# The guard of the softmax sums moved to ScalarE, the gelu of v kept in PSUM for its statistics, the early scaling by ScalarE

## The chip, the cores and the metric

The program runs on one core of a Trainium2 chip. A core has five engines that work through their own instruction queues in order: TensorE (PE; its weight loads are shown as PEld), VectorE (DVE), ScalarE (ACT), GpSimd (POOL) and SyncE (SP), which here only issues transfers. The metric is the device time of one execution in microseconds, as a median over runs.

## What is computed

For 8 batches of 8 heads with 576 positions and a head size of 64, causal attention with a bias that grows with a running sum of relu(s), and behind it a gated feed-forward network (gMLP) on the 512 columns that the 8 heads of a batch make:

```
cum    = cumsum(max(s, 0))
scores = q @ k.T / 8 + min(-(cum_i - cum_j), 0), masked causally
attn   = exp(scores - max);  attn = attn / (sum(attn) + 1e-9)
x      = attn @ v                              # 8 heads side by side: 576 x 512
h      = gelu_tanh(x @ w_in);  u, v = h[:, :512], h[:, 512:]
v_n    = (v - mean(v)) / sqrt(var(v) + 1e-6) * g_ln
out    = x + (u * (w_sg @ v_n + b_sg)) @ w_out
```

All of it is float32. From the ninth head on, float32 products are made of rounded parts (a high and a low part of each operand).

## The kernel before

**Attention, a head at a time.** `scores` makes five row tiles of scores in PSUM (`sc`, lines 295 to 298), VectorE adds the mask, writes the tile to SBUF (`p`) and takes its row minimum (`mn`, line 305), ScalarE takes the exponential in place and sums its rows into a column of `sum` (line 315, an ACTIVATE and an accumulator read). There are two sets of `p` tiles, used by even and odd heads. `norm` then adds 1e-9 to the five columns of sums (line 320, VectorE, 128x5), takes the reciprocal (`rs`, line 321, VectorE) and multiplies the `p` tiles by it in place (line 335). Which engine multiplies is read from a table, `ENG`: all five tiles by GpSimd from head 12 on (`'n': 'ggggg'`); in heads 0 to 11 the fourth entry of `'n0': 'gggvg'` gives the 128x448 tile to VectorE. `transposes` turns `p` on TensorE (`pt`, line 374), ScalarE and VectorE copy the result out of PSUM (`pa`, `pb`, `pd`), and `pv` multiplies it with v (`xx`, line 447) into `xr`.

**Feed-forward, a batch at a time.** `ffn(b)` starts when its eight heads are done and runs beside the next eight. It consists of units, each with a PSUM tile: five `v` units (`vm`, 128 or 64 rows by 512), and eight each of `u` (`um`), `s` (`sm`) and `o` (`om`, 128x288). All of them take their PSUM tile from one pool of three buffers (`ps_m`, tag `m`). A unit's tile is free for another unit when its last reader is through. In a `v` unit, `gelu2` runs Square (ScalarE, line 490), a multiply (VectorE, 491), Tanh (ScalarE, 492) and a last multiply (VectorE, 493), which is the last reader of `vm` and writes to the SBUF tile `vt`. Behind it come the statistics (`BN_STATS` line 535, `BN_AGGR` line 536), five small steps on GpSimd for one over the root (`rt`, lines 538 to 543), and `(vt - mean) * g_ln` on VectorE (line 544, inputs `vt` and `g_b`). From that, `vn` is made as a high part (ScalarE, 552) and a low part (GpSimd, 554 and 555; for the 64-row unit VectorE). The `s` units need `vn` of all five `v` units.

**What sets the order.** `place` gives each step a due time counted in heads, and the steps are run in that order to give the program. Within that, a scheduler that replays the program with its own costs (`schedule_with_timeline_sim=True`) decides in which order each engine's queue gets its instructions. An edit of one instruction can therefore change the order on all engines.

Of the kernel before, what the change touches and what calls it, by code (L numbers as in the profile page):

```python
# [13 lines left out]
AF = mybir.ActivationFunctionType  # L14
ALU = mybir.AluOpType
# [9 lines left out]
CH = S // 2  # L25
# [23 lines left out]
U2 = 7  # L49
ENG = {'k': 'sg', 'vs': 'sg', 'xs': 'gg', 'ln': 'sg', 'gt': 'sg', 'w': 'gg', 'ws': 'sv', 'n': 'ggggg', 'n0': 'gggvg', 'ws1': 'g'}  # L50
MT = 52.0
# [8 lines left out]
def tile_attn_gmlp(  # L60
# [12 lines left out]
    nc = tc.nc  # L73
# [244 lines left out]
    def norm(h, its, rs):  # L318
        c = slice(min(its), max(its) + 1)
        nc.vector.tensor_scalar(out=rs[:, c], in0=sums[h % 2][:, c], scalar1=1e-9, scalar2=None, op0=ALU.add)  # L320
        nc.vector.reciprocal(out=rs[:, c], in_=rs[:, c])  # L321
        for it in its:
# [11 lines left out]
            for po, pi, f in o:  # L334
                e.tensor_scalar(out=po, in0=pi, scalar1=f, scalar2=1.0, op0=ALU.mult, op1=ALU.mult)  # L335

# [144 lines left out]
    def ffn(b):  # L481
# [6 lines left out]

        def gelu2(ps, t, n):
            nc.scalar.activation(out=t, in_=ps, func=AF.Square)  # L490
            nc.vector.scalar_tensor_tensor(out=t, in0=t, scalar=1.0 / GA, in1=ps, op0=ALU.add, op1=ALU.mult)
            nc.scalar.activation(out=t, in_=t, func=AF.Tanh, scale=GC * GA)
            nc.vector.scalar_tensor_tensor(out=t, in0=t, scalar=1.0, in1=ps, op0=ALU.add, op1=ALU.mult)  # L493

        vn = {}

        def v_unit(tt, _):
# [30 lines left out]
            if tt == NT:  # L528
                nc.scalar.copy(out=t, in_=ps[r:P])
                nc.vector.tensor_tensor(out=ps[0:r], in0=ps[0:r], in1=t, op=ALU.add)  # L530
            gelu2(ps[0:r], t, 512)
            bs = moe.tile([P, 6], F32, name="bs", tag="bs", bufs=2)
            mv = moe.tile([P, 2], F32, name="mv", tag="mv", bufs=2)
            rt = moe.tile([P, 4], F32, name="rt", tag="rt", bufs=2)
            nc.vector.bn_stats(out=bs[0:r], in_=t)
            nc.vector.bn_aggr(out=mv[0:r], in_=bs[0:r])
# [6 lines left out]
            nc.gpsimd.tensor_tensor(out=y, in0=y, in1=z, op=ALU.mult)  # L543
            nc.vector.scalar_tensor_tensor(out=t, in0=t, scalar=mv[0:r, 0:1], in1=g_b[0:r],
                                           op0=ALU.subtract, op1=ALU.mult)
# [18 lines left out]
        def u_unit(ch, dt):  # L564
# [148 lines left out]
```

## Time and profile before

| | |
|---|---|
| median of 3 runs | 851.02 us (850.61 to 851.17) |
| the profiled execution | 852.92 us, its span 851.2 us |
| TensorE busy | 804.4 us (95%) |
| VectorE busy | 637.4 us (75%) |
| GpSimd busy | 613.5 us (72%) |
| ScalarE busy | 569.9 us (67%) |
| granted TensorE clock, mean | 0.982 |

The profile's page gives, for one execution, the busy time of each engine, the span in 40 slices, the chain of work that ended last, and groups of instructions. A group's row reads: line, engine, operation, what it writes and reads, shape, count, then busy microseconds, mean nanoseconds of one, and the idle time of the engine before it with what ended that. A matmul's end is modelled, so that neighbouring matmuls overlap in the record and a busy TensorE isn't TensorE at its peak.

### The profile page before, as it was taken

What the parts mean: (1) busy time and instruction counts of PE and PEld (TensorE: products, weight loads), DVE (VectorE), ACT (ScalarE), POOL (GpSimd) and SP (SyncE); (2) the same over time, 40 slices, a digit from 0 to 9 for tenths busy, and PEclk for the clock granted to TensorE, in tenths of its full rate; (3) what the DMA queues carried; (4) which work ended last, traced back from release to release, by engine and by line L of the source; (5) the groups of instructions that cost most, each with busy time, mean ns of one, the idle gap of its engine ahead of it and who ended that gap; (6) DMA issues with size and microseconds to landing.
All of it is one profiled execution on the core that took longest, in us unless ns stands there. A gap on an engine that the chain in (4) does not pass through costs nothing.

```text
span 851.2 us, 16858 instructions
## 1 busy us (share of the span) xinstructions
PE 804.4 (95%) x5161; PEld 701.7 (82%) x5161; DVE 637.4 (75%) x1882; ACT 569.9 (67%) x1544; POOL 613.5 (72%) x979
## 2 busy tenths in 40 slices
PE   6899999999999999999999998999999999998998
PEld 3445666889989997998889997999779997898788
DVE  5997569876797678866987678966987768865552
ACT  4676668865687676867887675767877676764340
POOL 4988669977678767767887777767786968674541
PEclk9899999999999999999999999999999999999999
DMA  7556544334433442435424443334534444220101
GB/s 220 175 167 182 142 105 122 78 90 123 109 81 95 118 124 71 109 90 143 134 64 110 124 115 88 89 87 127 141 97 100 119 107 111 59 62 22 34 7 56
DMA packets 69806, 89.31 MB, mean 105 GB/s; under 512 B 25954, under 2 KB 42212, under 8 KB 69716
## 3 DMA queue, kind: packets, MB, share of 16 engines
q1 hardware_dynamic: 69716, 88.23, 39.6%
q8 instruction: 41, 0.67, 0.4%
q14 instruction: 49, 0.40, 0.2%
HBM read 42.27 MB, written 9.73 MB: 61 GB/s over the span
## 4 chain that ended last, share of the span: by engine, by line
PE 71%; DVE 9%; POOL 6%; DMA 5%; ACT 5%; issue 3%; SPq 1%; ACTq 0%; POOLq 0%; DVEq 0%
PE om L604 11%; PE sm L585 11%; PE xx L447 10%; PE um L570 9%; PE pt L374 8%; PE vm L506 8%; PE sc L297 4%; PE sc L298 4%; DMA q<-k 2%; DVE p L305 2%; DMA wraw<-in_w_in 1%; POOL p L335 1%; PE sm L589 1%; PE sm L588 1%; ACT p L315 1%
## 5 line engine op out<-in xcount | busy, mean ns | idle before, releaser
L335 POOL TENSOR_SCALAR p<-p,rs 128x448 f32<-128x448 f32 (+4 forms) x372 | 182.2, 501 | 32.7 <-DVE rs L321 14.3
L315 ACT ACTIVATE p<-p,mn 128x448 f32<-128x448 f32 (+4 forms) x320 | 177.7, 557 | 25.9 <-DVE mn L305 23.7
L305 DVE CUSTOM_DVE_ANT_0 p<-sc,mask 64x64 f32<-64x64 f32 (+4 forms) x320 | 124.5, 422 | 40.4 <-PE pt L374 25.8
L374 PE MATMUL pt<-ident,p 128*128 128x128 f32 (+1 forms) x832 | 138.7, 281 | 5.5 <-DVE pal L93 2.0
L93 POOL TENSOR_TENSOR k<-raw,k 128x576 fp32r<-128x576 f32 x56 | 80.6, 1440 | 70.7 <-ACT k L88 31.2
L570 PE MATMUL um<-xs,wi 128*128 128x288 f32 x768 | 126.1, 305 | 1.5 <-DVE u L493 1.2
L585 PE MATMUL sm<-ws,vn 128*128 128x288 f32 x768 | 125.6, 302 | 1.2 <-DVE u L493 1.1
L604 PE MATMUL om<-gt,wo 128*128 128x288 f32 x768 | 125.5, 298 | 0.0
L374 PEld LDWEIGHTS pt<-ident,p 128*128 128x128 f32 (+1 forms) x832 | 96.5, 140 | 25.7 <-DVE pal L93 4.3
L570 PEld LDWEIGHTS um<-xs,wi 128*128 128x128 f32 x768 | 113.3, 195 | 4.7 <-DVE u L493 1.5
L585 PEld LDWEIGHTS sm<-ws,vn 128*128 128x128 f32 x768 | 110.2, 191 | 2.6 <-DVE u L493 2.1
L604 PEld LDWEIGHTS om<-gt,wo 128*128 128x128 f32 x768 | 110.5, 188 | 1.9 <-DVE ot L608 0.3
L506 PE MATMUL vm<-wi,xs 128*128 128x512 f32 x384 | 104.6, 404 | 3.9 <-POOL xs L90 2.2
L297 PE MATMUL sc<-k,q 128*128 128x448 f32 x336 | 100.9, 307 | 3.8 <-DVE mn L305 3.0
L298 PE MATMUL sc<-k,q 66*128 66x448 f32 x336 | 90.5, 299 | 0.5 <-DMA k<-cum 0.4
L506 PEld LDWEIGHTS vm<-wi,xs 128*128 128x128 f32 x384 | 69.5, 190 | 20.3 <-POOL xs L90 2.3
L88 ACT CAST pbh<-pt 128x512 fp32r<-128x512 f32 x104 | 49.1, 478 | 52.3 <-PE pt L374 51.7
L93 POOL TENSOR_TENSOR gt<-u,gt 128x288 fp32r<-128x288 f32 x64 | 50.9, 806 | 35.3 <-ACT gt L88 34.2
L297 PEld LDWEIGHTS sc<-k,q 128*128 128x128 f32 x336 | 60.8, 181 | 12.3 <-DVE mn L305 6.0
L93 DVE TENSOR_TENSOR pbl<-pt,pbh 128x512 fp32r<-128x512 f32 x104 | 56.0, 549 | 13.7 <-ACT pbh L88 13.6
L298 PEld LDWEIGHTS sc<-k,q 66*128 66x128 f32 x336 | 60.9, 181 | 6.0 <-issue 1.3
L315 ACT ACTIVATION_READ_ACCUMULATOR p<-p,mn 128x1 f32 (+1 forms) x320 | 60.5, 189 | 0.0
(142 smaller groups left out, 1723.4 us busy)
## 6 DMA issues: line engine op xcount, KB each, us to landing
q<-k SPq DMA_DIRECT2D x168, 144.0 KB
raw<-in_kq SPq DMA_DIRECT2D x56, 288.0 KB
vr<-in_vp SPq DMA_DIRECT2D x52, 192.0 KB
out_t<-ot SPq DMA_DIRECT2D x64, 144.0 KB
k<-k SPq DMA_DIRECT2D x56, 144.0 KB
wraw<-in_w_in SPq DMA_DIRECT2D x16, 256.0 KB
kf<-in_kq SPq DMA_DIRECT2D x8, 288.0 KB
qf<-in_kq SPq DMA_DIRECT2D x8, 288.0 KB
```

What stands on the lines that cost most here:

```text
L93: eng_lo.tensor_tensor(out=lo, in0=src, in1=hi.bitcast(F32), op=ALU.subtract)
L297: nc.tensor.matmul(o, d["q1"][:, i0:i0 + r], d["k1"][:, j0:j1], start=True, stop=False)
L298: nc.tensor.matmul(o, q2[h % 2][:, i0:i0 + r], d["k2"][0:66, j0:j1], start=False, stop=True)
L305: nc.vector.tensor_tensor_reduce(out=pbuf[h % 2][it][0:r, j0:j1], in0=pst[0:r, c0:c0 + j1 - j0], in1=(mask2 if it in (2, 4) else mask)[0:r ...
L315: nc.scalar.activation(out=p, in_=p, func=AF.Exp, bias=d["mn"][0:r, it:it + 1], scale=-1.0, accum_out=sums[h % 2][0:r, it:it + 1])
L335: e.tensor_scalar(out=po, in0=pi, scalar1=f, scalar2=1.0, op0=ALU.mult, op1=ALU.mult)
L374: nc.tensor.transpose(out=ps[0:n, c:c + P], in_=pb[it][:, jb:jb + n], identity=ident)
L447: nc.tensor.matmul(xx[0:rows, o0:o1], st(jt), m, **{"start": False, "stop": False, **kw})
L506: nc.tensor.matmul(ps[0:r], xs[c][:, xi, ts_], wi[:, c, wj, fs], start=(n == 0), stop=(n == 11))
L570: nc.tensor.matmul(ps[:, 0:CH], wi[:, c, wj, dt * P:(dt + 1) * P], xs[c][:, xi, cs], start=(n == 0), stop=(n == 11))
L585: nc.tensor.matmul(ps[:, 0:CH], vn[j][:, vi, ds_], ws[:, j, wj, cs], start=(n == 0), stop=False)
L604: nc.tensor.matmul(ps[:, 0:CH], wo[:, c, wj, ms], gt[ch, c][:, gi, :], start=(n == 0), stop=(n == 11))
```

## The change

Three edits. (1) Line 320, the sum plus 1e-9, is a ScalarE ACTIVATE (Copy with a bias) in place of a VectorE tensor_scalar. (2) In `n0` the entry `v` becomes `s`: in heads 0 to 11 the 128x448 tile of `p` is scaled by a ScalarE ACTIVATE (Copy with the column of `rs` as its scale). (3) In a `v` unit the last multiply of gelu writes back into the PSUM tile `vm`; the statistics and the step with the mean read it there. The last reader of `vm` is now line 544 (548 of the changed file), and that instruction reads one tile from PSUM and one, `g_b`, from SBUF.

```
-ENG = {..., 'n': 'ggggg', 'n0': 'gggvg', 'ws1': 'g'}
+ENG = {..., 'n': 'ggggg', 'n0': 'gggsg', 'ws1': 'g'}
...
     def norm(h, its, rs):
         c = slice(min(its), max(its) + 1)
-        nc.vector.tensor_scalar(out=rs[:, c], in0=sums[h % 2][:, c], scalar1=1e-9, scalar2=None, op0=ALU.add)
+        nc.scalar.activation(out=rs[:, c], in_=sums[h % 2][:, c], func=AF.Copy, bias=1e-9)
         nc.vector.reciprocal(out=rs[:, c], in_=rs[:, c])
...
             for po, pi, f in o:
-                e.tensor_scalar(out=po, in0=pi, scalar1=f, scalar2=1.0, op0=ALU.mult, op1=ALU.mult)
+                if e is nc.scalar:
+                    nc.scalar.activation(out=po, in_=pi, func=AF.Copy, scale=f)
+                else:
+                    e.tensor_scalar(out=po, in0=pi, scalar1=f, scalar2=1.0, op0=ALU.mult, op1=ALU.mult)
...
-        def gelu2(ps, t, n):
+        def gelu2(ps, t, last=None):
             nc.scalar.activation(out=t, in_=ps, func=AF.Square)
             nc.vector.scalar_tensor_tensor(out=t, in0=t, scalar=1.0 / GA, in1=ps, op0=ALU.add, op1=ALU.mult)
             nc.scalar.activation(out=t, in_=t, func=AF.Tanh, scale=GC * GA)
-            nc.vector.scalar_tensor_tensor(out=t, in0=t, scalar=1.0, in1=ps, op0=ALU.add, op1=ALU.mult)
+            nc.vector.scalar_tensor_tensor(out=t if last is None else last, in0=t, scalar=1.0, in1=ps,
+                                           op0=ALU.add, op1=ALU.mult)
...
-            gelu2(ps[0:r], t, 512)
+            gelu2(ps[0:r], t, ps[0:r])
...
-            nc.vector.bn_stats(out=bs[0:r], in_=t)
+            nc.vector.bn_stats(out=bs[0:r], in_=ps[0:r])
...
-            nc.vector.scalar_tensor_tensor(out=t, in0=t, scalar=mv[0:r, 0:1], in1=g_b[0:r],
+            nc.vector.scalar_tensor_tensor(out=t, in0=ps[0:r], scalar=mv[0:r, 0:1], in1=g_b[0:r],
                                            op0=ALU.subtract, op1=ALU.mult)
...
-            gelu2(ps[:, 0:CH], t, CH)
+            gelu2(ps[:, 0:CH], t)
```

The order of the queues moves too. Three places of it follow. The numbers in the names are those of buffers; line numbers of the changed file are up to four higher.

The first is VectorE's queue in the last batch, around the fourth-last `v` unit (`vm_11155`, `vt_11168`), when no head is left beside it. Before:

```order
L493 SCALAR_TENSOR_TENSOR vt_11168<-vt_11168,vm_11155 128x512
L491 SCALAR_TENSOR_TENSOR u2_11202<-u2_11202,um_11189 128x288
L535 BN_STATS bs_11173<-vt_11168 128x6
L491 SCALAR_TENSOR_TENSOR u2_11220<-u2_11220,um_11207 128x288
L493 SCALAR_TENSOR_TENSOR u2_11202<-u2_11202,um_11189 128x288
L536 BN_AGGR mv_11174<-bs_11173 128x2
L544 SCALAR_TENSOR_TENSOR vt_11168<-vt_11168,mv_11174,g_b_144 128x512
```

And in the change:

```order
L496 SCALAR_TENSOR_TENSOR vm_11155<-vt_11168,vm_11155 128x512
L494 SCALAR_TENSOR_TENSOR u2_11202<-u2_11202,um_11189 128x288
L539 BN_STATS bs_11173<-vm_11155 128x6
L494 SCALAR_TENSOR_TENSOR u2_11220<-u2_11220,um_11207 128x288
L496 SCALAR_TENSOR_TENSOR u2_11202<-u2_11202,um_11189 128x288
L540 BN_AGGR mv_11174<-bs_11173 128x2
L548 SCALAR_TENSOR_TENSOR vt_11168<-vm_11155,mv_11174,g_b_144 128x512
```

The order stands as it did; what moved is the last reader of `vm_11155`, from the first of these seven rows to the last.

The second is ScalarE's queue around the end of a head in the middle of the program (its last exponential is `p_1_4`, its sums are `sum_1`, its reciprocals `rs_4642`). Before:

```order
L315 ACTIVATE p_1_4_164,sum_1_165<-p_1_4_164,mn_4614 128x576
L88 CAST pah_4489<-pt_4484 128x512
L88 CAST pbh_4498<-pt_4493 128x512
L88 CAST gt_4797<-u2_4192 128x288
L88 CAST pbh_4498<-pt_4502 128x256
```

And in the change:

```order
L315 ACTIVATE p_1_4_164,sum_1_165<-p_1_4_164,mn_4614 128x576
L478 COPY xr_4080<-x0_4355 64x64
L495 ACTIVATE u2_4904<-u2_4904 128x288
L478 COPY xr_4080<-xx_4319 64x512
L88 CAST vs_4600<-vr_4364 128x6x64
L320 ACTIVATE rs_4642<-sum_1_165 128x5
L88 CAST pah_4489<-pt_4484 128x512
```

The new addition (L320) stands not right behind the exponential whose sum it takes, but behind four other ScalarE instructions. In 28 of the 64 heads one instruction stands between, in 19 two, in 17 three to five.

The third is TensorE's queue where head 32 begins, at the end of a batch's feed-forward. Before:

```order
L374 MATMUL pt_5155<-ident_124,p_0_4_153 128x128
L297 MATMUL sc_5459<-k1_5420,q1_5422 128x320
L298 MATMUL sc_5459<-k2_5421,q2_0_145 128x320
L297 MATMUL sc_5459<-k1_5420,q1_5422 128x192
L298 MATMUL sc_5459<-k2_5421,q2_0_145 128x192
L374 MATMUL pt_5164<-ident_124,p_0_3_151 128x128 x2
```

And in the change:

```order
L297 MATMUL sc_5459<-k1_5420,q1_5422 128x320
L298 MATMUL sc_5459<-k2_5421,q2_0_145 128x320
L297 MATMUL sc_5459<-k1_5420,q1_5422 128x192
L298 MATMUL sc_5459<-k2_5421,q2_0_145 128x192
L608 MATMUL om_5636<-gt_5257,wo_168 128x288 x3
L608 MATMUL om_5636<-gt_5289,wo_168 128x288 x3
L608 MATMUL om_5636<-gt_5398,wo_168 128x288 x3
L608 MATMUL om_5636<-gt_5417,wo_168 128x288 x3
L377 MATMUL pt_5164<-ident_124,p_0_3_151 128x128 x2
```

A whole `o` unit of the feed-forward stands there now between two pieces of attention. Counted over the queue, between the first transposes of neighbouring heads stand 3 to 68 feed-forward matmuls before (heads 24 to 40: 20, 66, 50, 48, 68, 62, 43, 17, 3, 39, 64, 39, 37, 46, 48, 58) and 30 to 58 in the change (31, 56, 36, 36, 42, 54, 58, 48, 30, 56, 36, 36, 42, 54, 58, 48). Behind the last matmul of the last head the two queues hold the same feed-forward units, but for a few places.

More of the change, by code (lines that the diff above doesn't have):

```diff
@@ L49 @@
 U2 = 7
-ENG = {'k': 'sg', 'vs': 'sg', 'xs': 'gg', 'ln': 'sg', 'gt': 'sg', 'w': 'gg', 'ws': 'sv', 'n': 'ggggg', 'n0': 'gggvg', 'ws1': 'g'}
+ENG = {'k': 'sg', 'vs': 'sg', 'xs': 'gg', 'ln': 'sg', 'gt': 'sg', 'w': 'gg', 'ws': 'sv', 'n': 'ggggg', 'n0': 'gggsg', 'ws1': 'g'}
 MT = 52.0
```

## The prediction

> **What bounds the kernel now.** I read the page first, its busy times and its chain.
>
> ```profile
> span 851.2 us, 16858 instructions
> PE 804.4 (95%) x5161; PEld 701.7 (82%) x5161; DVE 637.4 (75%) x1882; ACT 569.9 (67%) x1544; POOL 613.5 (72%) x979
> ...
> PE 71%; DVE 9%; POOL 6%; DMA 5%; ACT 5%; issue 3%; SPq 1%; ACTq 0%; POOLq 0%; DVEq 0%
> ```
>
> TensorE sets most of the end: 71% of the chain is its own work. Its queue is fixed and in order, so the other engines cost time where it stands and waits for them. Of VectorE's 637.4 us, 9% of 851.2 = 76.6 us lie on the chain, 12 parts in 100 of its work; of ScalarE 42.6 us of 569.9 (7.5%); of GpSimd 51.1 of 613.5 (8.3%). I use these shares below as the rate at which a microsecond on an engine becomes a microsecond of the end. It is an estimate.
>
> The groups by shape show the instructions that the change touches (columns: busy us, mean ns | idle before).
>
> ```profile
> L320 DVE TENSOR_SCALAR rs<-sum 128x5 f32<-128x5 f32 x64 | 29.0, 452 | 26.7 <-ACT p L315 25.7
> L321 DVE RECIPROCAL rs<-rs 128x5 f32<-128x5 f32 x64 | 11.8, 185 | 1.3
> L335 DVE TENSOR_SCALAR p<-p,rs 128x448 f32<-128x448 f32 x12 | 7.3, 609 | 0.1
> L544 DVE SCALAR_TENSOR_TENSOR vt<-vt,mv,g_b 128x512 f32<-128x512 f32 x32 | 31.1, 971 | 0.5
> L544 DVE SCALAR_TENSOR_TENSOR vt<-vt,mv,g_b 64x512 f32<-64x512 f32 x8 | 6.0, 755 | 0.1
> L535 DVE BATCH_NORM_STATS2 bs<-vt 128x6 f32<-128x512 f32 x32 | 21.9, 684 | 0.1
> L491 DVE SCALAR_TENSOR_TENSOR vt<-vt,vm 128x512 f32<-128x512 f32 x32 | 21.8, 682 | 8.7 <-ACT vt L490 8.5
> ```
>
> Five columns of sums take 452 ns, while the reciprocal on the same shape takes 185. Why, the timeline shows at two places.
>
> ```profile
> 242.25 1.29 POOL L555 TENSOR_TENSOR vn<-vt,vn 128x512 fp32r<-128x512 f32 x1
> 242.29 1.28 DVE L320 TENSOR_SCALAR rs<-sum 128x5 f32<-128x5 f32 x1
> ...
> 437.12 1.01 POOL L93 TENSOR_TENSOR vs<-vr,vs 128x384 fp32r<-128x384 f32 x1
> 437.25 1.44 DVE L544 SCALAR_TENSOR_TENSOR vt<-vt,mv,g_b 128x512 f32<-128x512 f32 x1
> 438.10 0.66 POOL L538 TENSOR_SCALAR rt<-mv 128x1 f32<-128x1 f32 x1
> ```
>
> The 128x5 addition begins 0.04 us behind a GpSimd instruction and ends 0.03 us behind its end: VectorE stands inside the instruction until GpSimd is through. At 437 the wait goes both ways: L544 ends late behind L93 on GpSimd, and GpSimd's next, tiny step, L538, is held until 438.76, where L544 ends (438.69). [...]
>
> **The change, part by part.** All against the profiled execution, 852.9 us (span 851.2 plus 1.7); the median shown, 851.0, lies 1.9 us under it.
>
> *VectorE loses work.* L320 goes whole: 29.0 us. Twelve L335 go: 7.3 us. The 40 L544 took 31.1 + 6.0 = 37.1 us; with one input in PSUM the nearest row is L491, 682 ns, and the pointer to the mean may keep it at the 64-row form's 755, so I take 740: 29.6 us, 7.5 less. Together 43.8 us, times 12% = 5.3 us. The statistics from PSUM keep their 684 ns, as L491 with a PSUM input takes no more than that. [...]
>
> *ScalarE gains work.*
>
> ```profile
> L315 ACT ACTIVATION_READ_ACCUMULATOR p<-p,mn 128x1 f32 x256 | 48.4, 189 | 0.0
> L315 ACT ACTIVATE p<-p,mn 128x448 f32<-128x448 f32 x64 | 42.6, 665 | 7.4 <-DVE mn L305 6.9
> L475 ACT COPY xr<-x 64x64 f32<-64x64 f32 x52 | 10.8, 208 | 8.9 <-PE x L469 7.0 <-DVE ot L608 0.8
> ```
>
> The addition lies between 189 and 208 ns: 64 x 0.20 = 12.8 us. The scaling of 448 columns with a pointer is nearest to the exponential of that shape, 665 ns: 12 x 0.67 = 8.0 us. 20.8 us times 7.5% = 1.6 us. The addition waits in a queue: up to five ScalarE instructions stand between it and its exponential, about half a microsecond each, and the reciprocal behind it holds VectorE's queue as L320 did (25.7 us of idle behind the exponentials). Behind the reciprocal waits GpSimd with the scaling of `p`. I put a later `rs` at nothing: among TensorE's waits no row names `p` of GpSimd, so the scaled tiles are ready before their transposes; if that cover were gone, a microsecond for each of 64 heads would show.
>
> *GpSimd is held less.*
>
> ```profile
> L538 POOL TENSOR_SCALAR rt<-mv 128x1 f32<-128x1 f32 (+1 forms) x40 | 18.2, 454 | 25.9 <-DVE mv L536 22.3 <-DVE rs L321 3.4
> L540 POOL TENSOR_TENSOR rt<-rt 128x1 f32<-128x1 f32 (+1 forms) x40 | 8.8, 221 | 2.6
> ```
>
> L538 should fall from 454 to the 221 ns of its neighbour: 40 x 0.23 = 9.3 us, times 8.3% = 0.8 us. So the port waits are worth 5.3 - 1.6 + 0.8 = **4.5 us**. From below the bound is nothing (all hidden under TensorE); from above, the 18.7 us that 64 additions spend over some 160 ns.
>
> *The buffers of PSUM are held longer.* A `v` tile is released after L544 in place of L493: at least 0.68 + 0.17 + 0.74 = 1.6 us later, and more with other work between. The last batch shows what hangs on it.
>
> ```profile
> 803.29 0.69 DVE L493 SCALAR_TENSOR_TENSOR vt<-vt,vm 128x512 f32<-128x512 f32 x1 [2.36 <-ACT vt L492]
> 803.89 0.45 DVE L491 SCALAR_TENSOR_TENSOR u<-u,um 128x288 f32<-128x288 f32 x1
> 804.03 3.05 PE L506 MATMUL vm<-wi,xs 128*128 128x512 f32 x12 [1.32 <-DVE vt L493]
> 804.25 0.69 DVE L535 BATCH_NORM_STATS2 bs<-vt 128x6 f32<-128x512 f32 x1
> 804.86 0.43 DVE L491 SCALAR_TENSOR_TENSOR u<-u,um 128x288 f32<-128x288 f32 x1
> 805.22 0.45 DVE L493 SCALAR_TENSOR_TENSOR u<-u,um 128x288 f32<-128x288 f32 x1
> 805.79 0.75 DVE L544 SCALAR_TENSOR_TENSOR vt<-vt,mv,g_b 128x512 f32<-128x512 f32 x1
> ...
> 810.41 1.61 PEld L570 LDWEIGHTS um<-xs,wi 128*128 128x128 f32 x12 [0.35 <-DVE vt L493]
> 812.55 0.73 DVE L544 SCALAR_TENSOR_TENSOR vt<-vt,mv,g_b 128x512 f32<-128x512 f32 x1
> ```
>
> All three buffers are held at 804, and the next `v` unit starts as L493 ends. In the change the first buffer to come free is that of a `u` unit, after 0.45 + 0.69 + 0.43 + 0.45 = 2.0 us; at 810.41 the same happens again, and there L544 ends 2.9 us later. One delay covers part of the other, and L538 starts the chain to `vn` half a microsecond sooner, so I take **2.5 us more** for the tail, between nothing and 4.9.
>
> In the other batches heads run beside the `v` units. TensorE's own list of waits:
>
> ```profile
> PE vm L506 <- DVE vt L493: 1.3, 1, 1.3
> PE um L570 <- DVE u L493: 1.2, 1, 1.2
> PE sm L585 <- DVE u L493: 1.1, 3, 0.4
> ```
>
> Only 3.6 us in all are spent on a buffer that gelu still holds, most of it in the tail just shown. The bounds for the 35 other `v` units are nothing and 35 x 1.6 = 56 us; the rows stand near the low end, since attention can stand in between. I take **2 us more**.
>
> *The order is more even.* Before, feed-forward work runs out between batches, as stretches of whole heads show (columns: us, PE busy, PEld, DVE, ACT, POOL).
>
> ```profile
> 353.50:367.00 13.50, 13.50 (x104) 13.36 (x103) 9.06 (x28) 9.58 (x27) 12.34 (x16) 1.00 0.36 89
> 390.60:399.30 8.70, 8.32 (x59) 7.30 (x58) 6.92 (x24) 6.98 (x21) 5.22 (x9) 1.00 0.56 142
> 399.30:407.20 7.90, 6.38 (x40) 4.87 (x39) 5.92 (x21) 6.87 (x20) 7.37 (x11) 1.00 0.54 138
> ...
> 309.10:407.20 98.10, 93.44 (x639) 85.48 (x638) 76.99 (x227) 71.10 (x193) 72.86 (x119) 1.00 0.41 106
> 407.20:502.80 95.60, 93.65 (x645) 87.65 (x644) 75.70 (x230) 70.80 (x193) 73.47 (x118) 0.98 0.43 109
> ```
>
> Head 28 has 68 feed-forward matmuls and its TensorE is full; head 32 has 3, and TensorE's loads are idle for 3 us of 7.9. Eight heads with such a hole take 98.1 us, the eight after them, whose work is spread better, 95.6 for the same matmuls. In the change every eight heads have the spread kind of order. Three such pairs lie between 195 and 785 us: 3 x 2.5 = 7.5 us at most by this row. That the replay which made the order knows nothing of these waits makes me take **5 us**; nothing is the lower bound, and three times the 1.4 + 3.0 us in which heads 31 and 32 leave TensorE's loads idle, 13 us, the upper.
>
> Sum: 852.9 - 4.5 - 5 + 2.5 + 2 = 847.9, and 1.9 less for the median: **846.0 us**.
>
> **Rivals.** *PSUM becomes the bound.* The longer hold isn't covered in the middle either: each of the seven other batches loses what one place of the tail loses, 2.0 us, so 14 us and 4.9 in the tail, against 4.5 of port waits and no gain by order: 851 + 14.4 = 865; at half that, 858. It decides from 7 us on, a fifth of a microsecond for each of 35 `v` units. For it: three buffers, and VectorE's queue puts up to 13 other instructions between gelu's end and L548 in the middle batches. Against it: the 3.6 us above.
>
> *Hidden anyway.* TensorE's 71% of the chain stays what it is, the port waits lay in slack, the tail's loss and the order's gain cancel: 851.
>
> *The wait moves.* The reciprocal, now the first of the pair on VectorE, waits for GpSimd in L320's place: 18.7 us of the 43.8 stay, 2.2 us at the end, 848. Against it: its mean of 185 ns, though GpSimd is 72% busy.
>
> *VectorE was the bound of the `v` stages.* There the waits count in full (18.7 us) and the even order gives 7.5, less the same 4.5: 851 - 21.7 = 829; with half the waits 839.
>
> **How the numbers follow.** Forecast 0.38, PSUM 0.29, hidden 0.13, the wait moves 0.08, VectorE the bound 0.12. About 0.2% (1.7 us) is what a measurement can tell from no change. Faster by more takes the forecast, the bound and most of the moved wait: 0.56; slower 0.29; the rest, 0.15, within. The range reaches from 836, between the two values of the last rival, to 858, the PSUM rival at half; what is left out is some 0.05 below and 0.14 above. The forecast's own range is 842 to 849.
>
> **What would show it.** Right: no L320 on VectorE; L548 near 740 ns with no long ones and L538 near 221; VectorE's busy time near 594 us and ScalarE's near 591; heads in the middle all between 9 and 15 us. Wrong: TensorE waiting for L548 in the middle of the program by several microseconds a batch, or a reciprocal of 400 ns; a tail longer than 66.2 us plus 5 (785 to the end now) would make the PSUM rival true even with the port waits gone.

## The result, and the profile after

The change takes **829.19 us** (826.72 to 830.11) against 851.1 (850.61 to 851.68) of the kernel before: a ratio of 0.9738, interval 0.9714 to 0.9761, 21.9 us. A second measurement gave 829.78 us and 0.9743 (0.9703 to 0.9782). The medians leave out an execution in a slow state, one of this second measurement and one of e3 below. Forecast were 846.0, between 836 and 858. The direction was right, the size was not: the time lies outside the range, at the value that the last rival gave (829).

The head of the page of the profile after, with its chain of waits (this execution took 829.98 us):

```profile
span 828.2 us, 16736 instructions
PE 794.3 (96%) x5161; PEld 695.6 (84%) x5161; DVE 597.6 (72%) x1806; ACT 577.4 (70%) x1620; POOL 597.6 (72%) x979
...
PE 73%; DVE 13%; DMA 6%; ACT 3%; issue 3%; POOL 2%; SPq 1%; DVEq 0%; POOLq 0%; ACTq 0%
```

VectorE lost 39.8 us of busy time, GpSimd 15.9. ScalarE's page figure grew by 7.5 only, though its two new rows below hold 21.1; the page counts time in which instructions overlap only once (ScalarE's rows by line add up to 663.3 us before and 684.8 after, where the page says 569.9 and 577.4). The groups by shape that answer to those of before:

```profile
L320 ACT ACTIVATE rs<-sum 128x5 f32<-128x5 f32 x64 | 13.1, 205 | 0.0
L336 ACT ACTIVATE p<-p,rs 128x448 f32<-128x448 f32 x12 | 8.0, 663 | 1.0 <-DVE rs L321 1.0
L321 DVE RECIPROCAL rs<-rs 128x5 f32<-128x5 f32 x64 | 11.6, 182 | 4.0 <-ACT rs L320 3.6
L548 DVE SCALAR_TENSOR_TENSOR vt<-vm,mv,g_b 128x512 f32<-128x512 f32 x32 | 23.7, 741 | 0.4
L548 DVE SCALAR_TENSOR_TENSOR vt<-vm,mv,g_b 64x512 f32<-64x512 f32 x8 | 5.9, 737 | 0.0
L539 DVE BATCH_NORM_STATS2 bs<-vm 128x6 f32<-128x512 f32 x32 | 22.1, 691 | 0.2
L542 POOL TENSOR_SCALAR rt<-mv 128x1 f32<-128x1 f32 (+1 forms) x40 | 8.9, 222 | 21.0 <-DVE mv L540 19.8 <-DVE xr L479 0.4
```

None of these rows of VectorE is drawn out by a wait for GpSimd any more: the longest L321 takes 192 ns, the longest L548 754, the longest L539 700. The two longest of TensorE's own waits for a buffer of the feed-forward's pool, from the view of waits (total, times, longest):

```profile
PE vm L510 <- DVE u L496: 2.2, 1, 2.2
PE um L574 <- DVE vt L548: 2.0, 1, 2.0
```

Where the time went, by stretches: up to the first transposes of head 7, to those of head 16, to those of the last head, and the tail behind them (columns as in the prediction; behind POOL stand the granted clock, the share of the DMA engines and GB/s). Before:

```profile
0.00:96.10 96.10, 82.14 (x327) 45.90 (x327) 74.03 (x235) 58.75 (x173) 71.96 (x107) 0.96 0.62 181
96.10:194.90 98.80, 93.21 (x560) 73.71 (x558) 75.62 (x234) 70.67 (x198) 78.59 (x124) 0.97 0.41 102
194.90:779.00 584.10, 566.14 (x3874) 524.89 (x3872) 453.03 (x1342) 417.44 (x1127) 436.43 (x701) 0.99 0.40 102
779.00:851.20 72.20, 62.91 (x408) 57.17 (x407) 34.71 (x73) 23.00 (x49) 26.50 (x49) 0.98 0.10 31
```

And after:

```profile
0.00:93.60 93.60, 80.63 (x328) 44.85 (x328) 67.71 (x219) 63.30 (x189) 70.30 (x107) 0.98 0.63 186
93.60:185.80 92.20, 87.82 (x537) 68.12 (x535) 68.34 (x218) 72.73 (x210) 72.35 (x119) 1.00 0.44 109
185.80:747.20 561.40, 554.77 (x3858) 517.14 (x3857) 425.40 (x1296) 416.86 (x1172) 428.49 (x704) 1.00 0.42 106
747.20:828.20 81.00, 71.04 (x447) 65.53 (x446) 36.15 (x75) 24.48 (x52) 26.46 (x51) 0.94 0.10 31
```

Of the 23.0 us, 9.1 are gone by head 16 and 22.7 in heads 16 to 62; the tail takes 8.8 more, with 39 more matmuls in it. Counted from the last matmul of the last head, the same 366 matmuls take 69.6 us after 66.0, so 3.6 of the 8.8 are loss and the rest is work that lay elsewhere. In the long stretch TensorE stood idle for 18.0 us before and for 6.6 now. That is half of the 22.7; the other half is busy time, 11.4 us less for 16 matmuls less. Behind a part of this second half stands the clock column: 0.99 has become 1.00, and 0.97 has become 1.00 in the stretch ahead of it. In the long stretch TensorE ran at half clock (0.50 or 0.51) four times for 3.41 us before and not once after, which by an estimate, half of 3.41 us for each, is worth up to 4 x 1.7 = 6.8 us. The mean clock over the whole execution was 0.982 before and is 0.992 now. So 851.2 x 0.018 = 15.3 us of clock were lost before and 828.2 x 0.008 = 6.6 now: up to 8.7 of the 23.0 us came by way of a clock of which the prediction says nothing. By the medians over the executions, 13.6 to 15.3 before and 6.6 to 7.5 in the change, it is 6 to 9 us.

### The profile page after: what moved, and what is told of

It is laid out like the page before. It is cut to its first block, busy times and chain, and to the rows that moved or that the text cites. A ratio compares the mean times of both kernels' runs of the same rounds, so it can differ in the third digit from the quotient of the medians.

```text
span 828.2 us, 16736 instructions
## 1 busy us (share of the span) xinstructions
PE 794.3 (96%) x5161; PEld 695.6 (84%) x5161; DVE 597.6 (72%) x1806; ACT 577.4 (70%) x1620; POOL 597.6 (72%) x979
## 4 chain that ended last, share of the span: by engine, by line
PE 73%; DVE 13%; DMA 6%; ACT 3%; issue 3%; POOL 2%; SPq 1%; DVEq 0%; POOLq 0%; ACTq 0%
PE om L608 12%; PE sm L589 11%; PE um L574 10%; PE vm L510 9%; PE xx L450 9%; PE pt L377 8%; PE sc L297 4%; PE sc L298 4%; DVE p L305 2%; DMA q<-k 2%; PE sm L593 1%; DMA xq<-xs 1%; PE sm L592 1%; DVE vm L496 1%; DVE wbits L220 1%
## 5 line engine op out<-in xcount | busy, mean ns | idle before, releaser
L338 POOL TENSOR_SCALAR p<-p,rs 128x448 f32<-128x448 f32 (+4 forms) x372 | 181.0, 500 | 30.5 <-DVE rs L321 10.9
L305 DVE CUSTOM_DVE_ANT_0 p<-sc,mask 64x64 f32<-64x64 f32 (+4 forms) x320 | 126.2, 422 | 55.3 <-PE pt L377 29.6
L377 PE MATMUL pt<-ident,p 128*128 128x128 f32 (+1 forms) x832 | 136.6, 278 | 4.6 <-DVE pbl L389 2.6
L574 PE MATMUL um<-xs,wi 128*128 128x288 f32 x768 | 124.1, 303 | 4.0 <-DVE vt L548 2.0
L93 POOL TENSOR_TENSOR k<-raw,k 128x576 fp32r<-128x576 f32 x56 | 80.6, 1439 | 63.7 <-ACT k L88 34.1
L574 PEld LDWEIGHTS um<-xs,wi 128*128 128x128 f32 x768 | 110.0, 191 | 10.3 <-DVE u L496 3.2
L510 PEld LDWEIGHTS vm<-wi,xs 128*128 128x128 f32 x384 | 71.6, 194 | 20.8 <-DVE u L496 2.4
L93 POOL TENSOR_TENSOR gt<-u,gt 128x288 fp32r<-128x288 f32 x64 | 50.9, 807 | 44.3 <-ACT gt L88 43.9
L93 DVE TENSOR_TENSOR pbl<-pt,pbh 128x512 fp32r<-128x512 f32 x104 | 56.6, 549 | 16.8 <-ACT pbh L88 16.7
L88 ACT CAST k<-raw 128x576 fp32r<-128x576 f32 x56 | 37.6, 671 | 38.8 <-PE sc L297 33.3
```

The costliest lines, as they stand in the source:

```text
L88: nc.scalar.copy(out=hi, in_=src)
L93: eng_lo.tensor_tensor(out=lo, in0=src, in1=hi.bitcast(F32), op=ALU.subtract)
L305: nc.vector.tensor_tensor_reduce(out=pbuf[h % 2][it][0:r, j0:j1], in0=pst[0:r, c0:c0 + j1 - j0], in1=(mask2 if it in (2, 4) else mask)[0:r ...
L377: nc.tensor.transpose(out=ps[0:n, c:c + P], in_=pb[it][:, jb:jb + n], identity=ident)
L510: nc.tensor.matmul(ps[0:r], xs[c][:, xi, ts_], wi[:, c, wj, fs], start=(n == 0), stop=(n == 11))
L574: nc.tensor.matmul(ps[:, 0:CH], wi[:, c, wj, dt * P:(dt + 1) * P], xs[c][:, xi, cs], start=(n == 0), stop=(n == 11))
```

## The experiments

Two theories stood against each other. "Port wait" stands below for what the prediction showed at 242 and 437 us: an instruction of VectorE or GpSimd that stands until one of the other engine is through. The name is the author's, as are "port" and "lock" wherever they stand: the traces show the standing (L320's 1.28 us beside GpSimd's 1.29, and 0.66 us of L538, whose shortest takes 0.21), and no run shows what in the hardware causes it. The reductions that are said to take no port took 159 to 161 ns (e5, e6, e12) and 652 (e15, 128x512). The guard is the addition of 1e-9. **WAITS**: the port waits that are gone were worth most of the 22 us, and the prediction's price for them was too low. **ORDER**: the more even spread of the feed-forward matmuls, which came with the change, is what gained. The table has all measurements. Its last column is the clock that was lost, the median over a kernel's executions of span x (1 - mean clock); the kernel before has 13.6 to 15.3 there.

| kernel | us | ratio to before (interval) | clock lost, us |
|---|---|---|---|
| the change, measured again (e18) | 829.78 | 0.9743 (0.9703 to 0.9782) | 7.5 |
| e2: the change, a locking step behind the guard | 835.15 | 0.9822 (0.9758 to 0.9886) | 5.8 |
| e13: the change, L548 from SBUF | 841.85 | 0.9870 (0.9824 to 0.9916) | 6.7 |
| e14: both | 846.80 | 0.9937 (0.9910 to 0.9964) | 10.1 |
| e3: before, more even order | 851.95 | 1.0012 (0.9973 to 1.0051) | 8.5 |
| e7: the change, less even order | 833.36 | 0.9809 (0.9782 to 0.9836) | 8.3 |
| e12: the change, guard as a reduction, most even order | 839.65 | 0.9857 (0.9814 to 0.9901) | 9.2 |
| e1: before, sums with a stride | 851.31 | 1.0008 (0.9974 to 1.0042) | 14.4 |
| e6: before, guard as a reduction | 846.44 | 0.9962 (0.9930 to 0.9994) | 11.8 |
| e4: gelu of v in PSUM alone | 843.00 | 0.9926 (0.9891 to 0.9961) | 10.9 |
| e5: e4 and guard as a reduction | 840.31 | 0.9891 (0.9868 to 0.9914) | 9.2 |
| e9: PSUM and guard, no early scaling | 837.62 | 0.9822 (0.9761 to 0.9883) | 7.5 |
| e8: guard on ScalarE alone | 855.15 | 1.0065 (1.0043 to 1.0088) | 13.7 |
| e10: early scaling alone | 869.72 | 1.0206 (1.0161 to 1.0250) | 22.6 |
| e11: guard and early scaling | 864.30 | 1.0152 (1.0100 to 1.0205) | 15.1 |
| e15: e11, L548 as a reduction | 847.26 | 0.9939 (0.9912 to 0.9966) | 8.9 |
| e16: e11, buffer of v held as in the change | 864.34 | 1.0150 (1.0112 to 1.0188) | 20.7 |
| e17: the change, last batch's gelu of v in SBUF | 825.53 | 0.9692 (0.9639 to 0.9745) | 6.2 |

Many of these times are not what either theory expected (the expectations follow): e2, e5, e6, e7 and e9 lie between the two, e8, e10, e11 and e12 above both, and e17 half a microsecond below both.

### The waits put back into the change's own order

In e2 the reciprocal is replaced by a VectorE multiplication of the same five columns, in the form that took 452 ns at line 320 in the kernel before, where the reciprocal took 185. In e13, L548 reads `vt` and `g_b`, two SBUF inputs, and writes to `vm`, so that `vm` is let go at the same place; the mean and `g_b` are then left out of the result, and `vn` no longer waits for L548 itself. e14 has both. Apart from these instructions the orders are those of the change, but for 24 (e13) and 46 (e2) rows of TensorE's queue.

```
e2, e14:
-        nc.vector.reciprocal(out=rs[:, c], in_=rs[:, c])
+        nc.vector.tensor_scalar(out=rs[:, c], in0=rs[:, c], scalar1=0.001, scalar2=None, op0=ALU.mult)
e13, e14:
-            nc.vector.scalar_tensor_tensor(out=t, in0=ps[0:r], scalar=mv[0:r, 0:1], in1=g_b[0:r],
+            nc.vector.scalar_tensor_tensor(out=ps[0:r], in0=t, scalar=mv[0:r, 0:1], in1=g_b[0:r],
```

> The changed kernel, except that the reciprocal on VectorE (line 321) is a multiplication of the same 128x5 columns by a constant, in the form that line 320 had before; the softmax isn't normalised, so the output is another. The queues keep the order of the change but for some rows in the first heads and in the tail (46 of about 5400 compared rows of TensorE). The 64 waits for GpSimd should be back, at L321, with about 450 ns each. Theory ORDER: at most 4 us over the changed kernel, 829 to 833. Theory WAITS: most of the gain is lost, 840 to 850.

> The changed kernel, in which L548 reads its two tiles from SBUF again (the tanh tile vt in place of vm, and g_b) and writes to vm, so that the buffer is held as long as in the change; the steps behind it read vt, so the mean and g_ln are left out and the output is another. The five queues are those of the change but for 24 rows of TensorE in the tail. L548 should be back at about 950 ns and GpSimd's step at 400. Theory WAITS: 837 to 845, the third edit's gain lost. Theory ORDER: 829 to 832.

> The changed kernel with both kinds of port waits back in its own order: L548 as in the run before, and the multiplication in place of the reciprocal as in the second run of this study; normalisation, mean and g_ln are left out. What is left of the 22 us after that is what the order and the move of work to ScalarE give. Theory WAITS: 843 to 851. Theory ORDER: 833 to 838, the 6 us that the lock of the guard cost alone and little more.

Measured against 829.19 us: e2 +6.0, e13 +12.7, e14 +17.6. The two prices add up (18.7 against 17.6). The first is the least certain: the interval of e2's ratio begins at 0.9758, where that of the change ends at 0.9761. The groups by shape of e2:

```profile
L321 DVE TENSOR_SCALAR rs<-rs 128x5 f32<-128x5 f32 x64 | 35.7, 558 | 0.9 <-ACT rs L320 0.5
L556 ACT ACTIVATE vn<-vt,rt 128x512 fp32r<-128x512 f32 x32 | 22.9, 716 | 2.1 <-POOL rt L547 2.1
```

Of e13:

```profile
L548 DVE SCALAR_TENSOR_TENSOR vm<-vt,mv,g_b 128x512 f32<-128x512 f32 x32 | 25.2, 786 | 0.4
L548 DVE SCALAR_TENSOR_TENSOR vm<-vt,mv,g_b 64x512 f32<-64x512 f32 x8 | 11.1, 1388 | 0.0
L542 POOL TENSOR_SCALAR rt<-mv 128x1 f32<-128x1 f32 x32 | 12.4, 387 | 17.1 <-DVE mv L540 16.2 <-DVE xr L479 0.4
L556 ACT ACTIVATE vn<-vt,rt 128x512 fp32r<-128x512 f32 x32 | 23.1, 723 | 16.0 <-POOL rt L547 16.0
```

Of the kernel before:

```profile
L552 ACT ACTIVATE vn<-vt,rt 128x512 fp32r<-128x512 f32 x32 | 23.1, 723 | 12.2 <-POOL rt L543 11.9
```

Of the change:

```profile
L542 POOL TENSOR_SCALAR rt<-mv 128x1 f32<-128x1 f32 x32 | 7.2, 224 | 19.2 <-DVE mv L540 17.9 <-DVE xr L479 0.4
L556 ACT ACTIVATE vn<-vt,rt 128x512 fp32r<-128x512 f32 x32 | 22.9, 717 | 4.9 <-POOL rt L547 4.9
```

In e2 VectorE stands 35.7 - 11.6 = 24.1 us longer in L321, and the end is 6.0 later: a quarter. In e13 VectorE stands (25.2 + 11.1) - (23.7 + 5.9) = 6.7 us longer in L548, and GpSimd some 6.1 us longer in L542 with its 64-row form (321 ns after 213): 12.8 us, and the end is 12.7 later by the medians, 9.2 between the two profiled executions. A microsecond of this wait costs 0.7 to a whole one.

Two paths lead from it to TensorE. By the first, L548 holds GpSimd's L542, the first of the steps that make `rt`, and ScalarE then waits 16.0 us for `rt` before it can make `vn` for the `s` units, against 4.9 in the change and 12.2 before; in e2 it waits 2.1. By the second, L548 is in the change's order the last reader of `vm`, so that a longer L548 lets the buffer go later. What TensorE's weight loads wait for tells how much each brings. In the change:

```profile
PEld um L574 <- DVE vt L548: 2.6, 2, 2.2
PEld vm L524 <- DVE vt L548: 0.8, 3, 0.3
PEld sm L589 <- ACT vn L556: 0.3, 1, 0.3
PEld sc L297 <- DVE mn L305: 3.6, 10, 0.8
```

In e13:

```profile
PEld um L574 <- DVE vm L548: 5.2, 7, 2.3
PEld vm L524 <- DVE vm L548: 3.9, 4, 1.1
PEld sm L589 <- ACT vn L556: 2.9, 5, 0.6
```

In e2:

```profile
PEld sc L297 <- DVE mn L305: 8.0, 18, 0.8
```

This is idle time of the weight loads, not all of it lost at the end, but the proportion is clear: the buffer brings 9.1 - 3.4 = 5.7 us more in e13, `vn` 2.6. The second path is the larger one. In e2 neither grows by more than 1.2; there the weight loads for the scores wait 4.4 us more for VectorE's row minimum, which comes later with the rest of VectorE's queue. The kernel before lets `vm` go after gelu, ahead of L544, so the second path does not exist there, and what the wait of L544 cost in that kernel is not measured.

Where it costs, the windows of five and then three heads show (heads 48 to 52, 53 to 55). The change:

```profile
574.20:631.70 57.50, 56.57 (x379) 50.94 (x377) 49.64 (x150) 47.67 (x133) 44.76 (x81) 1.00 0.45 113
631.70:667.72 36.02, 36.02 (x268) 34.92 (x267) 22.29 (x72) 23.50 (x69) 27.38 (x38) 1.00 0.43 109
```

e14:

```profile
584.16:645.41 61.25, 58.26 (x379) 52.36 (x377) 52.91 (x148) 48.03 (x133) 47.60 (x81) 0.97 0.43 106
645.41:681.44 36.03, 36.03 (x268) 34.93 (x267) 23.00 (x74) 23.47 (x69) 27.63 (x38) 1.00 0.42 109
```

The last three heads of eight take 36.0 us with and without the waits: TensorE is busy all the time and hides them. The first five, which hold most of the `v` and `u` units, pay. Worked out from the starts of all heads 16 to 62, e14 loses 12.4 us to the change, all of it in the first five heads of each eight and 0.0 in the other three. WAITS holds here: 17.6 of the 21.9 us.

How one wait, here that of the sums, became 3.3 us shows at head 50. First VectorE in e14, then in the change at the same place of the program:

```profile
610.42 1.49 DVE L321 TENSOR_SCALAR rs<-rs 128x5 f32<-128x5 f32 x1
...
614.56 0.78 DVE L548 SCALAR_TENSOR_TENSOR vm<-vt,mv,g_b 128x512 f32<-128x512 f32 x1
```

```profile
599.98 0.19 DVE L321 RECIPROCAL rs<-rs 128x5 f32<-128x5 f32 x1
...
603.26 0.75 DVE L548 SCALAR_TENSOR_TENSOR vt<-vm,mv,g_b 128x512 f32<-128x512 f32 x1
```

Then a weight load of TensorE in e14, and the clock in windows around that place:

```profile
615.55 0.19 PEld L524 LDWEIGHTS vm<-wi,xq 128*128 128x128 f32 x1 [1.50 <-DVE vm L548]
```

```profile
615.30:617.50 2.20, 1.46 (x7) 1.13 (x8) 2.20 (x8) 1.09 (x4) 1.69 (x7) 1.00 0.26 61
617.50:619.20 1.70, 1.70 (x8) 1.50 (x8) 0.04 (x1) 1.24 (x2) 0.77 (x2) 0.56 0.18 40
619.20:620.90 1.70, 1.70 (x9) 1.50 (x9) 0.00 (x0) 0.41 (x1) 1.20 (x1) 0.50 0.00 0
```

L321 stands 1.49 us, until GpSimd's L93 is through at 611.88. All that VectorE does behind it comes later: L548 ends at 615.34, 4.9 us after L321 began, against 4.0 in the change. The weight load of TensorE's next `v` matmul waits for L548, and the matmul starts at 615.58 after 1.21 us of idling; a second idling of 0.45 us follows. Then the clock falls to a half for 3.4 us, and head 50 takes 15.8 us in place of 12.5.

### The order

The spread is set by a number of the planner, the same for every batch; 54 makes it more even, 51 less.

```
e3: the kernel before, e12: the change with the reduction of e6
-MT = 52.0
+MT = 54.0
e7: the change
-MT = 52.0
+MT = 51.0
```

> The kernel before with one number of the planner's table altered: the total by which a batch's feed-forward work is spread over the due times, 54 in place of 52. No instruction is added, removed or moved to another engine; the order is another: between the first transposes of neighbouring heads in the middle stand 21 to 61 feed-forward matmuls (before 3 to 68, in the change 30 to 58). All waits for GpSimd stay. Theory ORDER: most of the gain, 830 to 840. Theory WAITS: 849 to 853.

> The changed kernel with the planner's total at 51 in place of 52: the same instructions on the same engines, in an order with one head of 5 feed-forward matmuls in each eight (5, 51, 48, 43, 37, 68, 51, 57) in place of 30 to 58. Theory ORDER: 837 to 845. Theory WAITS: 827 to 832.

> The change with the guard as the reduction over two columns on VectorE, which takes no port and gives ScalarE nothing, and with the planner's total at 54, which gives an order of 27 to 59 feed-forward matmuls a head that repeats every eight. If ScalarE's 13 us for the guard cost anything at the end it is faster than the change: 824 to 829. If what counts is that L320 leaves VectorE's queue whole, or the particular order: 830 to 838.

The kernel before with 21 to 61 feed-forward matmuls between first transposes, in place of 3 to 68, is no faster: 851.95 us, ratio 1.0012. The change with 5 to 68 loses 4 us of its 22. The most even one of all, 27 to 59, is 10 us slower than the change, though its guard, a reduction on VectorE, differs as well. Evenness alone gains nothing here, and e7 leaves at most 4 us to the more even order of the change.

### The guard by itself

```
e1: the sums lie two apart, so that VectorE reads them with a stride
-        t = const.tile([P, 5], F32, name=f"sum_{i}")
+        t = const.tile([P, 5, 2], F32, name=f"sum_{i}")
...
-        sums.append(t)
+        sums.append(t[:, :, 0])
e6 (before), e5 (with gelu of v in PSUM): 1e-9 lies beside each sum, and a reduction adds the two
...
-        nc.vector.tensor_scalar(out=rs[:, c], in0=sums[h % 2][:, c], scalar1=1e-9, scalar2=None, op0=ALU.add)
+        nc.vector.tensor_reduce(out=rs[:, c], in_=sums[h % 2][:, c, :], op=ALU.add, axis=mybir.AxisListType.X)
```

> The kernel before, except that the five sums of a head stand in every second column of their tile (128x5x2), so that line 320 reads with a stride. The order of all five queues is that of before, row for row. If the stride keeps L320 from waiting for GpSimd, its mean falls from 452 to about 160 to 200 ns and the port waits of the guard are gone in the order of before. Theory ORDER (the change gained by spreading feed-forward work evenly over the heads): the time stays within 4 us of before, 847 to 851. Theory WAITS (the change gained because VectorE no longer stands behind GpSimd): most of the 22 us comes here too, 830 to 840. If L320 still takes about 450 ns, the run says nothing on either.

> The kernel before with that same reduction for line 320: the guard doesn't wait for GpSimd and ScalarE gets nothing. The waits of L544 stay. The order of the queues is that of before up to about head 38 and shifted by heads after it, with the same pattern (3 to 69 feed-forward matmuls a head). Theory WAITS: 844 to 846, 6 us less than before. Theory ORDER: 849 to 853.

> The third edit alone, as in the run before, and in it the guard without a port wait and without ScalarE: the tile of sums gets a second column of 1e-9 for each sum, and line 320 is a reduction over the two columns on VectorE. The queues stand as in the run with the third edit alone but for 46 rows of TensorE, nearly all in the first heads. L320 should take about 160 to 190 ns without waits, 17 us less on VectorE. Theory WAITS (in a fixed order each us of guard wait is worth a third at the end, as the locked reciprocal showed with 6 us for 24): 843 to 836 to 838. Theory ORDER: 841 to 845.

The rows of e1 and of e6:

```profile
L320 DVE TENSOR_SCALAR rs<-sum 128x5 f32<-128x5 f32 x64 | 29.8, 465 | 26.3 <-ACT p L315 25.6
```

```profile
L320 DVE TENSOR_REDUCE rs<-sum 128x5 f32<-128x10 f32 x64 | 10.3, 161 | 25.6 <-ACT p L315 25.4
```

The stride did not take the wait away (465 ns), so e1 tells nothing of either theory. The reduction did (161 ns): 18.7 us less on VectorE, 3 to 4 us at the end, and 2.7 with the PSUM edit in place (843.0 to 840.3; there the row falls from 420 to 159 ns). With e2's 6.0 that is three values for the guard's wait, 2.7 to 6 us, at a rate of 0.16 to 0.25. e2 and e5 keep nearly the order that they are compared with; e6 keeps that of before only up to about head 38.

### The three edits one by one

Each of these is the kernel before with the edits named, as the change's diff has them; e9 has `'n0': 'gggvg'` again, e10 line 320 as before and gelu of v in SBUF.

> The third edit alone: gelu of v stays in PSUM; the guard and the early scaling stay on VectorE. Its order has 15 to 68 feed-forward matmuls a head, without a head of 3, in a pattern that repeats after 16 heads. Theory ORDER: about half of the gain, 836 to 844. Theory WAITS: only the waits of L544 and L538 are gone, a third of all, 843 to 848. If the longer hold of the buffers costs what the first rival said: 853 to 860.

> The change without its second edit: the scaling of the 128x448 tile in heads 0 to 11 stays on VectorE, guard on ScalarE and gelu of v in PSUM. From head 26 on the counts of feed-forward matmuls a head are those of the change (30, 56, 36, 36, 42, 54, 58, 48); before that they differ. Theory SUM (the edits add up as they do alone: -7.5 for PSUM, +5 for the guard): 846 to 850. Theory TOGETHER (guard and PSUM help only together, because the scheduler then makes the order that repeats every eight heads): 830 to 836, and heads 24 to 56 take 374 to 376 us as in the change.

> The first edit alone: the guard on ScalarE, the rest as before; its order has 3 to 75 feed-forward matmuls a head. Theory WAITS: 6 us less than before, 843 to 846, as with the reduction in the run above. Theory ORDER: 849 to 853, since the holes are still there.

> The second edit alone: in heads 0 to 11 the 128x448 tile is scaled by ScalarE. Its order has 3 to 66 feed-forward matmuls a head. Theory SUM: what the change gains over the sum of the other two must be this edit, 10 us or more: 836 to 841. Theory TOGETHER: 7 us leave VectorE in the first 130 us, head 12 comes 1 to 4 us sooner, 847 to 850.

> The change without its third edit: guard and early scaling on ScalarE, gelu of v in SBUF, so the waits of L548 for GpSimd and of GpSimd's step for VectorE are back. Its order has 15 to 75 feed-forward matmuls a head. Theory SUM: 7.5 us over the change, 836 to 838. Theory TOGETHER: near the guard alone, 848 to 855.

Gelu of v in PSUM alone gives 8 us, with the guard 13 to 14, with early scaling 22. The other two edits without it make the kernel slower: guard 4, early scaling 18, both 13 us. These kernels differ from one another in the order of all queues, so that the steps can't be read as prices of the edits. The rows of e11, where no wait is meant to be added:

```profile
L548 DVE SCALAR_TENSOR_TENSOR vt<-vt,mv,g_b 128x512 f32<-128x512 f32 x32 | 29.0, 907 | 0.5
L548 DVE SCALAR_TENSOR_TENSOR vt<-vt,mv,g_b 64x512 f32<-64x512 f32 x8 | 8.7, 1082 | 0.2
```

They wait as long as those of before did (37.7 us in all, 37.1 before), and yet the kernel is 13 us slower. That asked for two more.

### The wait or the hold

e11 differs from the change in two things: L548 waits again, and `vm` is let go earlier, after gelu. In e15 L548 is a reduction over an axis of one element, of the same size, which writes `vt` (the mean and `g_b` are left out), and the hold is that of e11. In e16 the wait stays and a copy of one column of `vm` behind L548 holds the buffer as in the change.

```
e15, against e11:
-            nc.vector.scalar_tensor_tensor(out=t, in0=t, scalar=mv[0:r, 0:1], in1=g_b[0:r],
-                                           op0=ALU.subtract, op1=ALU.mult)
+            nc.vector.tensor_reduce(out=t, in_=t.rearrange("p (n o) -> p n o", o=1), op=ALU.max, axis=mybir.AxisListType.X)
e16, against e11, behind the same two lines:
+            nc.vector.tensor_copy(out=rt[0:r, 3:4], in_=ps[0:r, 0:1])
```

> The change without its third edit (864 us), in which L548 is a reduction over an axis of one element: one input from SBUF, no port, 128x512 in and out; the mean and g_ln are left out. The hold of the buffers is that of before. Theory WAITS: 845 to 855, since the waits that the third edit removed are gone here too. Theory ORDER: 858 to 868, with a pattern of 3 to 72 feed-forward matmuls a head.

> The guard on ScalarE and early scaling of the change, gelu of v in SBUF (so L548 keeps two SBUF inputs and its wait), and one added VectorE copy of a single PSUM column behind L548, so that the PSUM buffer of v is held as long as in the change. It leaves nothing out. The copy adds 40 short instructions (estimate from the 10 to 25 ns of DVE's smallest rows plus issue: 40 x 0.06 = 2.4 us). WAITS (port waits are the price): 860 to 870, as the same edits without the copy (864.3). ORDER (what made that one slow is the shorter hold and the order that follows from it): 835 to 850.

Without the wait 847.26 us, 17.0 less than e11; with the wait and the longer hold 864.34, as e11 (its copies, 150 ns each, are 6 us of VectorE's time besides). The rows of e15 and of e16:

```profile
L548 DVE TENSOR_REDUCE vt<-vt 128x512 f32<-128x512 f32 x32 | 20.9, 652 | 0.0
```

```profile
L548 DVE SCALAR_TENSOR_TENSOR vt<-vt,mv,g_b 128x512 f32<-128x512 f32 x32 | 29.6, 924 | 0.5
```

These two don't settle the question, because the scheduler gave each an order of its own: e15 has 3 to 72 feed-forward matmuls a head where e11 has 15 to 75, and TensorE's rows in the traces differ from those of e11 in more than a thousand places in both (22 for e13 against the change). The 17.0 us therefore hold the wait, a shorter instruction (at most 40 x 0.09 = 3.6 us) and another order, and no price of the wait or of the hold by itself follows from them. What they do show is how much else there is: e15, with no wait in either place, is still 17 to 18 us behind the change. This part isn't explained.

### The tail

In the last batch no head runs beside the `v` units, and no GpSimd step of a head. There gelu of v stays in SBUF, as in the kernel before.

```
+            vs_ = t if b == B - 1 else ps[0:r]
-            gelu2(ps[0:r], t, ps[0:r])
+            gelu2(ps[0:r], t, vs_)
...
-            nc.vector.bn_stats(out=bs[0:r], in_=ps[0:r])
+            nc.vector.bn_stats(out=bs[0:r], in_=vs_)
...
-            nc.vector.scalar_tensor_tensor(out=t, in0=ps[0:r], scalar=mv[0:r, 0:1], in1=g_b[0:r],
+            nc.vector.scalar_tensor_tensor(out=t, in0=vs_, scalar=mv[0:r, 0:1], in1=g_b[0:r],
```

> The changed kernel, in which the last batch alone keeps gelu of v in SBUF, so that its buffers are released as before. The queues are those of the change but for 23 rows of TensorE in the tail. If the longer hold costs the tail what the forecast said: 2 to 3 us less than the change, 826 to 827. If the tail has other work to do in that time: within 1 us of the change.

> The change once more, nothing edited, for the comparison with the version whose last batch keeps gelu of v in SBUF. Every theory: 826 to 832, ratio 0.971 to 0.977 to the kernel before.

825.53 us, 3.7 to 4.3 less than the change. Of all versions this is the fastest. Its tail, and the change's at the first of the three places where its clock falls:

```profile
744.80:822.00 77.20, 68.48 (x448) 62.92 (x446) 35.78 (x75) 24.14 (x52) 28.49 (x51) 0.98 0.10 33
```

```profile
757.40:760.82 3.42, 1.27 (x12) 1.16 (x10) 1.36 (x3) 0.79 (x2) 0.69 (x2) 0.99 0.00 0
760.82:764.23 3.41, 3.38 (x9) 2.47 (x10) 0.51 (x1) 0.90 (x2) 1.39 (x1) 0.50 0.12 43
```

The others stand at 777.88 and 788.12. e17's tail is 3.8 us shorter than the change's 81.0, and its clock is 0.98 in place of 0.94: 77.2 x 0.02 against 81.0 x 0.06, 3.3 us. The change's two waits of 2.2 and 2.0 us for a buffer, shown above, end about where the second and the third stretch at half clock begin; in e17 the waits at these places take 0.6 and 1.2 us, and the clock stays whole. The runs don't tell how much of the 3.8 us is wait and how much is clock.

## Why the prediction was wrong

*The durations* were right: L548 741 and 737 ns (forecast 740), L542 222 (221), the addition on ScalarE 205 (200), the scaling 663 (670), VectorE's busy time 597.6 us (594). That L548 with one input in PSUM would neither wait for GpSimd nor hold it, on which 7.5 us of VectorE's and 9.3 of GpSimd's behind the forecast's 4.5 rest, no run had shown; in the change L548 took 724 to 754 ns and L542 209 to 236. ScalarE's is 577.4 where 591 was forecast. Heads 24 to 62 take 9.9 to 14.0 us, as was forecast, and none of the signs named for "wrong" came. So the signs tested the durations and not the rate at which they count.

*The step that failed is the rate* at which a microsecond on an engine becomes one of the end, "12 parts in 100", taken from VectorE's share of the chain. With it all that VectorE and GpSimd lose was worth 5.3 + 0.8 = 6.1 us, and of this the waits 2.2 + 1.7 = 3.9. Put back at the change's own order the waits cost 17.6. The rate is no property of an engine. The guard's wait was forecast at 18.7 x 0.12 = 2.2 us and costs 2.7 to 6. The wait of L548 and L538 was forecast at 7.5 x 0.12 + 0.8 = 1.7 us and costs 12.7, because each microsecond of it counts for 0.7 to 1. The prediction had a row that points there, L544 and L538 holding each other at 437 us, and did not follow it on: L538 is the first step to `rt`, and ScalarE's `vn` waited 12.2 us for that. Nor did it join the wait with the longer hold: in the change L548 lets `vm` go, and in e13 this is the larger path. The chain shows only what ended last in one execution; what it names under TensorE can itself be late because of VectorE, and it shows nothing of a clock.

*The order* was put at 5 us for its evenness. Evenness alone gains nothing (e3, e12), and e7 leaves it at most 4. The step from the kernel before to e14 holds all that came with the change except the waits: the order, the work that left VectorE, ScalarE's load, the hold and the tail. It takes 4.3 us off, where (10.3 + 7.3) x 0.12 + 5 - 1.6 - 4.5 = 1.0 was forecast. Most of these 4.3 us is clock: span times mean clock, as a median over the executions, is 835.6 us for both, and e14 loses 10.1 to the half clock where before lost 13.6. So 17.6 - 3.9 = 13.7 us of the miss of 16.9 lie in the waits and the other 3.2 here.

*The longer hold.* In the tail 2.5 us was near (3.6 behind the last head, 3.7 to 4.3 by e17), though a part of it is clock. In the other batches 2 us was too much: TensorE's matmuls wait for L548 once in the whole program, in the tail, and of the 3.4 us that its weight loads wait for L548 1.2 lie in the middle.

*The rivals.* "PSUM becomes the bound" falls with the time itself and with these 2.0 and 3.4 us. "Hidden anyway" falls with e14. "The wait moves to the reciprocal" falls by its 182 ns. "VectorE was the bound of the `v` stages" gave 829 and is the nearest: in heads 16 to 62 the cost lies in those with most of the `v` and `u` units and nowhere else. Its working was off all the same: it counted the guard's 18.7 us in full and the even order at 7.5, where it is L548's wait that counts nearly in full, the guard's a sixth to a quarter, and the order by its evenness 4 us at most. That the sum came out was luck.

*What stays open.* What the wait of L544 cost in the order of the kernel before, where it held no buffer; no run takes it out there with the order kept. Why e15 is 17 to 18 us slower than the change, and e8, e10 and e11 slower than the kernel before, though hardly any wait for GpSimd was added to them. Their queues differ from the change's in many places at once, and no run here takes a single one of these apart.

## What to carry to other kernels

Price a wait by the chain it stands in, not by its engine's share of the longest chain: follow the late result to the next engine and the next, follow the buffer that the waiting instruction holds, and ask whether TensorE is full there. Put a removed wait back into the new kernel, at the new kernel's order, before crediting it; edits compared each at an order of its own differed here by 10 to 20 us for other reasons. Read the clock beside the idle time: in e14 a window with 1.21 and 0.45 us of idling of TensorE stood ahead of 3.4 us at half clock.

## What the runs showed of the hardware that was not expected

**TensorE's clock fell to a half behind windows in which TensorE was busy for about half of the time.** In the kernel before, one place of the middle, with the window ahead and the 3.41 us behind it:

```profile
439.80:443.21 3.41, 1.94 (x11) 1.47 (x12) 3.41 (x13) 3.11 (x11) 3.24 (x9) 1.00 0.57 121
443.21:446.62 3.41, 3.41 (x16) 3.37 (x15) 2.74 (x11) 2.49 (x6) 2.08 (x4) 0.50 0.00 0
```

Five more such stretches start at 159.87, 176.94, 528.55, 637.77 and 723.11. In the profiles of the kernel before and of the change they last 3.41 us, once 6.83, and begin on a grid of the shorter step (from 443.21 to 528.55 it is 25 steps). The full-speed window of 3.41 us ahead of one had TensorE busy for 0.35 to 0.57 of its time there. The other windows of these two profiles, from 10 us on, had it busy for 0.58 or more. In e14 the 1.21 and 0.45 us of standing idle lie in the window ahead of one. By an estimate, half of 3.41 us, each such stretch cost up to 1.7 us. The profile of the change has none between 30 and 757 us, the kernel before has six. The clock is also a part of the spread between executions of one kernel: the kernel before took spans of 845.9 to 856.6 us beside e13, at mean clocks of 0.988 and 0.976, and 845.9 x 0.988 and 856.6 x 0.976 are both 836; over all 19 of those executions the products still spread over 7.5 us, the spans over 10.7.

**What waited for GpSimd and what did not.** The 128x5 addition waited with contiguous and with strided sums (452 ns in the kernel before, where its shortest took 156, and 465 in e1); a reduction that writes the same five columns did not (159 ns in e5 and e12, 161 in e6), and the reciprocal did not (179 to 187 ns as a mean in every kernel that keeps it). In the change the statistics from PSUM took 691 ns, 7 more than from SBUF in the kernel before, and L548 took 724 ns at least and 737 in the median with one input in PSUM, against 730 and 752 with both in SBUF in the kernel before.
